# A new order of works and more idle matmuls at the start of a fused linear-attention and softplus MLP kernel

## The chip, the cores and the metric

The kernel runs on one core of a Trainium2 chip. A core has TensorE (PE in the profile), VectorE (DVE), ScalarE (ACT), GpSimd (POOL) and SyncE (SP), which here issues nearly all DMAs. The metric is the device time of one execution in microseconds, the median of several runs.

## The reference

```python
def _attn_ref(q, k, v, omega):          # (8, 8, 576, 64), omega (128, 64)
    scale = 1.0 / np.sqrt(np.sqrt(D))
    q_s, k_s = (q * scale, k * scale)
    def phi(x):
        h = np.einsum('bhsd,md->bhsm', x, omega) - np.sum(x * x, -1, keepdims=True) / 2.0
        return np.exp(h - np.max(h, axis=-1, keepdims=True)) / np.sqrt(m)
    q_p, k_p = (phi(q_s), phi(k_s))
    kv = np.einsum('bhsm,bhsd->bhmd', k_p, v)
    z = np.sum(k_p, axis=2)
    num = np.einsum('bhsm,bhmd->bhsd', q_p, kv)
    den = np.einsum('bhsm,bhm->bhs', q_p, z)[..., None] + 1e-06
    return num / den
def _moe_ref(x, w_in, w_out):           # x (4608, 512), w_in (512, 2048)
    h = x @ w_in
    g = np.maximum(h, 0.0) + np.log1p(np.exp(-np.abs(h)))
    return g @ w_out
```

The output of the attention, with heads side by side, is the x of the MLP.

## The kernel before, in words

The attention is done in 16 quads (8 batches, two halves of the heads each). A quad's keys and queries come in five units of 128 tokens (the last is a tail of 64). For the two quads of batch 0, whose names carry `_0_` and `_1_` in the rows of the order, a key unit is loaded (`xk`), squared on ACT or POOL, projected on PE (`ppk`, L659, in row mode: two 64-row matmuls run side by side), reduced and biased on DVE (`smk`, L649 to L721), exponentiated on ACT (L729) and summed into `kt` on PE (L869). Query units (`xq`, `ppq`) follow in the same way, then transposes (`tpq`), the numerator (`nuq`, L985), the division and the transpose back (`xfq`), which gives the MLP input as a high and a low float32r part (`xh`, `xl`).

The MLP goes in blocks of 512 tokens (the first two of 256). One layer step is twelve matmuls of layer 1 (high by high, high by low, low by high, L1217 to L1219), a softplus on ACT and DVE (`u`, `gh`, `gl`), and three matmuls of layer 2 for each 128 tokens (L1277 to L1279). The weights come raw (`rawi`, `rawo`) and are split into the two parts by ACT, DVE and POOL during the first 100 us.

All of this is cut into some 4,900 works. A work is a piece of program for one engine, with a planned cost. Works are issued in the order of the table `ORDER`: an entry is twice the number of a work, plus one where its second engine is to be taken. A planner (`in_order`, then `timed`) goes through the table with planned costs, among them `START` (when an engine begins), `SLOW` (before this time PE works cost double), `change` (the price of a mode change of PE: plain, row mode "r", column mode "c") and `LULL`/`LULLED` (a pause of SP). It gives out buffers and PSUM banks in that order, so the table sets both who comes first on each engine and which buffer a work waits for. `with_fill` looks at the planned times: where PE is planned to pause it puts in idle matmuls (`fill`, L1733) on a free bank; each is a plain float32 matmul of the identity, which the trace shows as two instructions. Five more stand before the first work, on a zeroed tile `idle`. The planned costs don't run on the chip; only the order, the buffers and the idle matmuls do.

Of the kernel before, what the change touches and what calls it, by code (L numbers as in the profile page):

```python
# [19 lines left out]
P = 128  # L20
S = 576
D = 64
M = 128
NU = 5
DM = 512
# [9 lines left out]
START = {"SP": 0.65, "ACT": 2.1, "PE": 3.4}  # L35
SLOW = 7.9
LULL, LULLED = 20.7, 0.9
# [298 lines left out]
def change(old, new):  # L336

    if old == new:
        return 0.0
    return {("r", None): 0.08, ("c", None): 0, (None, "r"): 0.4, (None, "c"): 0.29}.get((old, new), 0.185)  # L340
# [85 lines left out]
def with_fill(out, held, banks, until, emit):  # L426

    last, all_ = None, []
    for i, w in enumerate(out):
        if w.engine == "PE":  # L430
# [6 lines left out]
            if names and n > 0:  # L437
                all_.append((emit, names[0], n))
# [1404 lines left out]
```

## Time and profile before

| | us |
|---|---|
| median of 3 runs | 993.84 |
| lowest and highest | 993.62 and 993.91 |
| the profiled execution | 996.06 |
| its span, from the first to the last instruction | 994.2 |
| PE busy | 982.4 |
| DVE busy | 799.1 |
| ACT busy | 703.8 |

The span lies 1.9 us below the profiled execution's own time, which lies 2.2 us above the median. Busy times count an engine's instructions as the profile models them; a PE that is busy is not yet one that does useful work, because idle matmuls count too.

### The profile page before, as it was taken

To read this page: it belongs to the slowest core of one execution; us is meant where nothing else is said; L and a number is where in the kernel's file an instruction comes from. 1 tells how busy PE (TensorE), PEld (TensorE's weight loads), DVE (VectorE), ACT (ScalarE), POOL (GpSimd) and SP (SyncE) were. 2 spreads that over 40 slices of the span, in tenths; PEclk is the share of its full clock that TensorE was granted. 3 is DMA by queue.
4 is the path that set the end of the run, shared out by engine and by line. 5 is a ranking of instruction groups with operands and counts; after the bars stand their busy time and mean duration, and the time that the engine had idled before them with its cause. 6 is when DMAs were issued, how large, how long until landed. Compare 5 with 4: busy or idle time off the path is not lost.

```text
span 994.2 us, 17161 instructions
## 1 busy us (share of the span) xinstructions
PE 982.4 (99%) x5553; PEld 808.9 (81%) x5553; DVE 799.1 (80%) x2141; ACT 703.8 (71%) x1708; POOL 314.5 (32%) x284
## 2 busy tenths in 40 slices
PE   9999999999999999999999999999999999999998
PEld 7888888888888788888888888887788778788887
DVE  6999987888888887798889898788877856999620
ACT  5999976768777786877776786877587635775610
POOL 3334333232345333335233431533331212221100
PEclk9999999999999999999999999999999999999999
DMA  9954454334443424342342433343441331000011
GB/s 338 403 188 158 154 152 121 116 110 120 122 130 95 152 77 138 118 139 84 103 150 83 115 117 106 113 134 104 128 133 44 93 109 43 1 1 1 1 32 53
DMA packets 64769, 113.82 MB, mean 114 GB/s; under 512 B 18316, under 2 KB 37672, under 8 KB 64680
## 3 DMA queue, kind: packets, MB, share of 16 engines
q1 hardware_dynamic: 64520, 112.60, 35.8%
q8 instruction: 44, 0.72, 0.3%
q14 instruction: 45, 0.37, 0.1%
q10 hardware_dynamic: 160, 0.13, 0.1%
HBM read 85.68 MB, written 27.03 MB: 113 GB/s over the span
## 4 chain that ended last, share of the span: by engine, by line
PE 83%; DVE 7%; ACT 5%; DMA 3%; issue 1%; SPq 0%; POOL 0%; DVEq 0%; ACTq 0%; POOLq 0%
PE acc L1277 12%; PE acc L1278 12%; PE acc L1279 12%; PE h L1217 10%; PE h L1218 9%; PE h L1219 9%; PE xp L1146 3%; PE kt L824 3%; PE pb L1551 2%; PE ppk L684 2%; PE ppq L684 2%; PE pa L1551 1%; DMA xq<-q 1%; PE pc L1551 1%; PE h L1393 1%
## 5 line engine op out<-in xcount | busy, mean ns | idle before, releaser
L1277 PE MATMUL acc<-wo,gh 128*128 128x512 f32 x512 | 203.6, 398 | 0.1
L1278 PE MATMUL acc<-wo,gh 128*128 128x512 f32 x512 | 200.5, 392 | 0.0
L1279 PE MATMUL acc<-wo,gl 128*128 128x512 f32 x512 | 199.5, 390 | 0.0
L1217 PE MATMUL h<-xh,wi 128*128 128x512 f32 (+1 forms) x512 | 189.2, 369 | 0.5 <-DVE u L1232 0.5
L1218 PE MATMUL h<-xl,wi 128*128 128x512 f32 (+1 forms) x512 | 186.5, 364 | 0.3 <-DVE xl L1018 0.3
L1219 PE MATMUL h<-xh,wi 128*128 128x512 f32 (+1 forms) x512 | 185.7, 363 | 0.0
L1240 POOL TENSOR_TENSOR gl<-u,gh 128x512 fp32r<-128x512 f32 (+1 forms) x74 | 89.0, 1203 | 148.2 <-ACT gh L1236 58.4
L1277 PEld LDWEIGHTS acc<-wo,gh 128*128 128x128 f32 x512 | 96.3, 188 | 22.6 <-issue 4.1
L1217 PEld LDWEIGHTS h<-xh,wi 128*128 128x128 f32 x512 | 96.5, 189 | 20.9 <-issue 3.3
L1279 PEld LDWEIGHTS acc<-wo,gl 128*128 128x128 f32 x512 | 96.1, 188 | 20.8
L1278 PEld LDWEIGHTS acc<-wo,gh 128*128 128x128 f32 x512 | 96.5, 188 | 15.8
L1219 PEld LDWEIGHTS h<-xh,wi 128*128 128x128 f32 x512 | 96.5, 188 | 15.6
L1218 PEld LDWEIGHTS h<-xl,wi 128*128 128x128 f32 x512 | 96.7, 189 | 14.1 <-DVE xl L1018 0.5
L1223 ACT ACTIVATE u<-h 128x512 f32<-128x512 f32 (+1 forms) x128 | 71.3, 558 | 45.8 <-PE h L1219 38.3
L1232 DVE SCALAR_TENSOR_TENSOR u<-h,u 128x512 f32<-128x512 f32 (+1 forms) x128 | 78.0, 616 | 14.9 <-ACT u L1229 13.5
L1065 POOL TENSOR_TENSOR phq<-phq,dnq 128x512 f32<-128x512 f32 x39 | 41.4, 1067 | 135.5 <-DVE dnq L1061 129.6
L1056 DVE CUSTOM_DVE_ANT_0 junk<-phq,zb 128x128 bf16<-128x128 f32 (+1 forms) x228 | 70.6, 310 | 11.2
L1226 ACT ACTIVATE u<-u 128x512 f32<-128x512 f32 (+1 forms) x128 | 75.7, 592 | 2.7
L1229 ACT ACTIVATE u<-u 128x512 f32<-128x512 f32 (+1 forms) x128 | 75.1, 590 | 2.9
L706 ACT ACTIVATE phk<-phk,smk 128x128 f32<-128x128 f32 x208 | 66.7, 391 | 6.7 <-DVE smk L721 6.5
L677 POOL TENSOR_TENSOR spq<-xq,spq 64x512 fp32r<-64x512 f32 (+1 forms) x29 | 37.8, 1304 | 97.7 <-ACT spq L673 78.5
L706 ACT ACTIVATE phq<-phq,smq 128x128 f32<-128x128 f32 x194 | 60.8, 393 | 4.9 <-DVE smq L721 4.8
(221 smaller groups left out, 2021.5 us busy)
## 6 DMA issues: line engine op xcount, KB each, us to landing
xk<-kx SPq DMA_DIRECT2D x28, 512.0 KB, 3.7
xq<-qx SPq DMA_DIRECT2D x28, 512.0 KB, 3.5
fdq<-flq SPq DMA_DIRECT2D x28, 512.0 KB, 2.8
qq<-fdq SPq DMA_DIRECT2D x112, 128.0 KB, 3.0
rawi<-wi SPq DMA_DIRECT2D x16, 512.0 KB, 7.7
rawo<-wo SPq DMA_DIRECT2D x16, 512.0 KB, 5.2
out<-o SPq DMA_DIRECT2D x32, 256.0 KB, 3.2
v<-vv SPq DMA_DIRECT2D x14, 576.0 KB, 4.3
```

The source lines that it names most:

```text
L706: nc.scalar.activation(x, x, AF.Exp, bias=b["sm"][:, 2, c : c + 1])
L1217: nc.tensor.matmul(b["h"], wh, xh[:, cc, t], start=cc == 0, stop=False)
L1218: nc.tensor.matmul(b["h"], wh, xl[:, cc, t], start=False, stop=False)
L1219: nc.tensor.matmul(b["h"], wl, xh[:, cc, t], start=False, stop=cc == NCC - 1)
L1223: nc.scalar.activation(b["u"], b["h"], AF.Abs)
L1226: nc.scalar.activation(b["u"], b["u"], AF.Exp, scale=-1.0)
L1229: nc.scalar.activation(b["u"], b["u"], AF.Ln, bias=1.0)
L1232: nc.vector.scalar_tensor_tensor(b["u"], b["h"], 0.0, b["u"], ALU.max, ALU.add)
L1240: (nc.vector if e == "DVE" else nc.gpsimd).tensor_tensor(b["gl"], b["u"], b["gh"].bitcast(F32), ALU.subtract)
L1277: nc.tensor.matmul(dst, gh, w2[fc][:, 0, c], start=start, stop=False, **kw)
L1278: nc.tensor.matmul(dst, gh, w2[fc][:, 1, c], start=False, stop=False, **kw)
L1279: nc.tensor.matmul(dst, gl, w2[fc][:, 0, c], start=False, stop=stop, **kw)
```

## The change

The change alters four things. The table `ORDER` is replaced as a whole. The planner's prices change: the start of SP, `LULLED`, the mode changes (and these are no longer doubled before `SLOW`), the first big load, and the layer steps, by under 1%. `with_fill` counts idle matmuls otherwise: before `EARLY` one for each 0.2 us of planned pause, without the doubled price; after 16 us the margin is 0.12 us in place of 0.25 us. And an idle matmul that stands between two row-mode works, like the seven (before: five) at the start, takes 64 rows of the identity in place of 128, so that it is of the row mode too.

```diff
-START = {"SP": 0.65, "ACT": 2.1, "PE": 3.4}
+START = {"SP": 0.85, "ACT": 2.1, "PE": 3.4}
 SLOW = 7.9
-LULL, LULLED = 20.7, 0.9
+EARLY = 8.6
+LULL, LULLED = 20.7, 0.5
...
 ORDER = (
-    384, 394, 386, 410, 415, 418, 434, 437, 390, 392, 416, 396, 420, 398, 422, 400, 402, 424, 426, 456, 478, 500, 522,
+    384, 386, 394, 391, 410, 418, 415, 434, 440, 456, 478, 500, 522, 388, 0, 392, 396, 416, 398, 400, 402, 404, 420,
...
-    return {("r", None): 0.08, ("c", None): 0, (None, "r"): 0.4, (None, "c"): 0.29}.get((old, new), 0.185)
+    return {("r", None): 0, ("c", None): 0, (None, "r"): 0.38, (None, "c"): 0.22}.get((old, new), 0.16)
...
-        w.engine, w.cost = e, w.on[e] + (change(mode, w.mode) if e == "PE" else 0)
-        w.cost *= 2 if e == "PE" and t < SLOW else 1
+        w.engine, w.cost = e, w.on[e] * (2 if e == "PE" and t < SLOW else 1)
+        w.cost += change(mode, w.mode) if e == "PE" else 0
...
-    last, all_ = None, []
+    last, mode, all_ = None, None, []
...
-            n = int((t - last - (0.05 if t < 16 else 0.25)) / (0.43 if t < SLOW else 0.224)) if last is not None and t < until else 0
+            n = 0
+            if last is not None and t < until:
+                n = int((t - last) / 0.2) if t < EARLY else int((t - last - (0.05 if t < 16 else 0.12)) / 0.224)
...
-                all_.append((emit, names[0], n))
-            last = w.end
+                all_.append((emit, names[0], n, mode == w.mode == "r"))
+            last, mode = w.end, w.mode
...
-            "SP", dma(P * 4 * cols) + (1.6 if early and kind == "k" and u == 1 and not q.qd else 0), load, behind=prev.get("load"),
+            "SP", dma(P * 4 * cols) + (1.75 if early and kind == "k" and u == 1 and not q.qd else 0), load, behind=prev.get("load"),
...
-                "PE", 0.684, lambda tt=tt: layer2(tt), after=[l, done_w["o", fc]], behind=box.get("l2"),
+                "PE", 0.682, lambda tt=tt: layer2(tt), after=[l, done_w["o", fc]], behind=box.get("l2"),
...
-    def fill(tag, n, idle=ident):
-        t = bank("fill", tag)[:, :P]
+    def fill(tag, n, half, idle=ident):
+        t, x = bank("fill", tag)[:, :P], idle[: D if half else P]
         for _ in range(n):
-            nc.tensor.matmul(t, idle, idle, start=True, stop=True)
+            nc.tensor.matmul(t, x, x, start=True, stop=True)
...
-        fill("at.0", 5, idle)
+        fill("at.0", 7, True, idle)
```

On PE the program begins before as follows. `ppk_a_u` is the projection of key unit u of quad a, four matmuls each, of which two stand here.

```order
L1733 MATMUL fill<-idle 128x128 x5
L659 MATMUL ppk_0_0_0_103<-omf,xk_0_0_101 128x128
...
L659 MATMUL ppk_1_0_0_113<-omf,xk_1_0_110 128x128
...
L1733 MATMUL fill<-ident 128x128 x2
L659 MATMUL ppk_0_1_0_150<-omf,xk_0_1_119 128x128
...
L659 MATMUL ppk_1_1_0_179<-omf,xk_1_1_135 128x128
...
L1733 MATMUL fill<-ident 128x128 x2
L659 MATMUL ppk_0_2_0_188<-omf,xk_0_2_137 128x128
...
L1733 MATMUL fill<-ident 128x128 x4
L659 MATMUL ppk_1_2_0_199<-omf,xk_1_2_139 128x128
```

After the change the same stretch of PE reads:

```order
L1735 MATMUL fill<-idle 128x128 x7
L661 MATMUL ppk_0_0_0_106<-omf,xk_0_0_103 128x128
...
L1735 MATMUL fill<-ident 128x128
L661 MATMUL ppk_1_0_0_117<-omf,xk_1_0_113 128x128
...
L1735 MATMUL fill<-ident 128x128 x9
L661 MATMUL ppk_0_1_0_136<-omf,xk_0_1_124 128x128
...
L661 MATMUL ppk_1_1_0_186<-omf,xk_1_1_142 128x128
...
L1735 MATMUL fill<-ident 128x128 x2
L661 MATMUL ppk_0_2_0_195<-omf,xk_0_2_144 128x128
...
L1735 MATMUL fill<-ident 128x128 x4
L661 MATMUL ppk_1_2_0_214<-omf,xk_1_2_146 128x128
```

The works stand in the same order. There are seven idle matmuls in place of five at the start, one new one between the first two units, and nine in place of two ahead of unit `0_1`; from `1_1` on the idle matmuls are as many as before. Behind these rows both programs have two idle matmuls, `ppk_0_3`, one idle matmul and the first `kt`.

At the first layer step PE has, before, a query projection (`ppq_1_3`) and a transpose ahead of the six matmuls of the first half of layer 1 (`h_0`):

```order
L985 MATMUL nuq_1_0_605<-kvs_1_585,xq_1_0_209 128x65 x4
L985 MATMUL nuq_1_1_612<-kvs_1_585,xq_1_1_273 128x65 x4
L659 MATMUL ppq_1_3_0_620<-omf,xq_1_3_320 128x128
...
L1001 MATMUL xfq_1_0_628<-ident,xq_1_0_209 128x128 x2
L1217 MATMUL h_0_645<-xh,wi_312 128x256
...
L985 MATMUL nuq_0_2_653<-kvs_0_446,xq_0_2_275 128x65 x4
L1001 MATMUL xfq_1_1_661<-ident,xq_1_1_273 128x128 x2
```

After the change the same works stand like this:

```order
L987 MATMUL nuq_1_0_614<-kvs_1_571,xq_1_0_240 128x65 x4
L987 MATMUL nuq_1_1_622<-kvs_1_571,xq_1_1_303 128x65 x4
L987 MATMUL nuq_0_2_627<-kvs_0_460,xq_0_2_305 128x65 x4
L1219 MATMUL h_0_637<-xh,wi_331 128x256
...
L1003 MATMUL xfq_1_0_654<-ident,xq_1_0_240 128x128 x2
L1003 MATMUL xfq_1_1_683<-ident,xq_1_1_303 128x128 x2
L661 MATMUL ppq_1_3_0_687<-omf,xq_1_3_392 128x128
```

Layer 1 begins ahead of the transpose `xfq_1_0` and of `ppq_1_3`, and the numerator of a third query unit has moved up before it.

## Rows read from the trace of the kernel before

**Rows 1.** The page: span; busy time, share and instructions of each engine.

```profile
span 994.2 us, 17161 instructions
...
PE 982.4 (99%) x5553; PEld 808.9 (81%) x5553; DVE 799.1 (80%) x2141; ACT 703.8 (71%) x1708; POOL 314.5 (32%) x284
```

**Rows 2.** Windows; busy us (instructions), then granted clock, DMA share, GB/s.

```profile
8.00:18.00 10.00, 9.83 (x58) 8.24 (x58) 5.33 (x19) 7.33 (x25) 2.89 (x6) 1.00 1.03 401
18.00:27.00 9.00, 8.77 (x77) 7.67 (x76) 8.12 (x29) 6.08 (x19) 3.38 (x5) 1.00 1.04 398
27.00:40.00 13.00, 12.21 (x112) 10.62 (x111) 11.91 (x40) 13.00 (x39) 4.73 (x6) 1.00 1.03 405
40.00:100.00 60.00, 57.51 (x471) 48.95 (x471) 58.01 (x169) 59.58 (x167) 21.94 (x20) 1.00 0.59 210
100.00:500.00 400.00, 399.04 (x2360) 329.67 (x2361) 338.93 (x948) 305.05 (x757) 145.33 (x127) 1.00 0.40 121
500.00:850.00 350.00, 349.21 (x1829) 283.72 (x1828) 286.31 (x764) 241.81 (x572) 111.55 (x95) 1.00 0.34 103
850.00:988.00 138.00, 137.42 (x607) 112.71 (x606) 85.41 (x156) 68.72 (x130) 23.36 (x21) 1.00 0.04 12
```

**Rows 3.** Waits of PE after 100 us: total us, times, longest.

```profile
PE ppk L684 <- DVE spk L677: 0.6, 1, 0.6
PE h L1217 <- DVE u L1232: 0.5, 1, 0.5
PE ppq L684 <- DVE phq L697: 0.4, 2, 0.3
PE ppk L684 <- DVE phk L697: 0.3, 1, 0.3
```

**Rows 4.** Timeline of PE, first 18 us: start, us, instruction, [idle before].

```profile
1.05 2.50 PE L1733 MATMUL fill<-idle 128*128 128x128 f32 x10 [1.05 <-DVE marks L488]
3.94 2.29 PE L659 MATMUL ppk<-omf,xk 64*128 64x128 f32 x16 [0.39 <-DMA xk<-k]
6.16 1.22 PE L1733 MATMUL fill<-ident 128*128 128x128 f32 x4
7.94 2.10 PE L659 MATMUL ppk<-omf,xk 64*128 64x128 f32 x16 [0.56 <-DMA xk<-k]
9.96 1.22 PE L1733 MATMUL fill<-ident 128*128 128x128 f32 x4
11.24 1.29 PE L659 MATMUL ppk<-omf,xk 64*128 64x128 f32 x8
12.46 2.07 PE L1733 MATMUL fill<-ident 128*128 128x128 f32 x8
14.60 1.29 PE L659 MATMUL ppk<-omf,xk 64*128 64x128 f32 x8
15.82 1.13 PE L1733 MATMUL fill<-ident 128*128 128x128 f32 x4
17.01 0.78 PE L659 MATMUL ppk<-omf,xk 64*128 64x128 f32 x8
...
20.20 0.94 PE L659 MATMUL ppk<-omf,xk 64*128 64x128 f32 x12
```

**Rows 5.** Timeline of PE at 59 us: the same idle matmul later.

```profile
59.46 0.83 PE L1733 MATMUL fill<-ident 128*128 128x128 f32 x6
```

**Rows 6.** Timelines of ACT and POOL: squares that start when a load lands.

```profile
7.83 0.42 ACT L642 ACTIVATE xk<-xk 128x256 f32<-128x256 f32 x1 [2.43 <-DMA xk<-k]
...
9.78 0.42 ACT L642 ACTIVATE xk<-xk 128x256 f32<-128x256 f32 x1 [0.51 <-DMA xk<-k]
8.84 0.61 POOL L644 TENSOR_TENSOR xk<-xk 128x256 f32<-128x256 f32 x1 [4.00 <-DMA xk<-k]
10.81 0.61 POOL L644 TENSOR_TENSOR xk<-xk 128x256 f32<-128x256 f32 x1 [1.36 <-DMA xk<-k]
12.10 0.46 ACT L642 ACTIVATE xk<-xk 128x256 f32<-128x256 f32 x1
```

**Rows 7.** Waits of DVE and of ACT between 8 and 27 us.

```profile
DVE smk L709 <- PE ppk L659: 4.9, 5, 1.5
ACT xk L729 <- DVE smk L721: 2.8, 1, 2.8
ACT xk L729 <- PE ppk L659: 1.9, 2, 1.2
```

**Rows 8.** Timeline at the end: the last matmul.

```profile
990.15 0.28 PE L1279 MATMUL right<-wo,g 128*128 128x256 f32 x1
```

More of the change, by code (lines that the diff above doesn't have):

```diff
@@ L346, in in_order @@
     free = {n: (0.0, None) for names in room.values() for n in names}
-    port, mode, lull, out = 0.0, None, LULLED, []
+    port, mode, lull, out = 0.0, "r", LULLED, []
     for k in ORDER:
@@ L386, in timed @@
     clock, head, ready, done = {e: START.get(e, 0.0) for e in queues}, dict.fromkeys(queues, 0), {}, set()
-    ports, mode, lull = {"DVE": -1.0, "POOL": -1.0}, None, LULLED
+    ports, mode, lull = {"DVE": -1.0, "POOL": -1.0}, "r", LULLED
     while len(done) < len(out):
@@ L406, in timed @@
         if e == "PE":
-            w.cost += change(mode, w.mode)
-            w.cost *= 2 if t < SLOW else 1
+            w.cost = w.cost * (2 if t < SLOW else 1) + change(mode, w.mode)
             mode = w.mode
@@ L1250, in plan_step @@
             a = do(
-                "PE", 0.70 if n < TB else 1.36, lambda ccs=ccs: layer1(ccs), after=[x for cc, x in need if cc in ccs] + [done_w["i", fc]], behind=a,
+                "PE", 0.70 if n < TB else 1.37, lambda ccs=ccs: layer1(ccs), after=[x for cc, x in need if cc in ccs] + [done_w["i", fc]], behind=a,
                 take=[] if ccs[0] else [("h", b, "hs")],
@@ L1398, in plan_plain @@
                 a = do(
-                    "PE", 1.36, lambda ccs=ccs: layer1(ccs), after=[x for cc in ccs for x in ready[t][cc]], behind=a,
+                    "PE", 1.37, lambda ccs=ccs: layer1(ccs), after=[x for cc in ccs for x in ready[t][cc]], behind=a,
                     take=[] if ccs[0] else [("h" if t == t7 else "bank", b, "hs")], give=[(w_box["i", fc], "w")] if t == t8 and ccs[0] else [],
@@ L1557, in plan_product @@
                 box["l1"] = do(
-                    "PE", 1.36, lambda: product(k, key, start), after=after, behind=box["l1"],
+                    "PE", 1.37, lambda: product(k, key, start), after=after, behind=box["l1"],
                     take=[("bank", b, ("bank", key))] if start else [], give=give,
@@ L1620, in plan_both @@
                 box["l2"] = do(
-                    "PE", 0.684, lambda tt=tt, fc=fc: layer2(t7, tt, fc), after=[gs[t7, fc][1], done_w["o", fc]],
+                    "PE", 0.682, lambda tt=tt, fc=fc: layer2(t7, tt, fc), after=[gs[t7, fc][1], done_w["o", fc]],
                     behind=box["l2"], take=[] if fc else [("acc", box, ("acc", i, tt))], give=[(gs[t7, fc][0], "gs")] if tt == 3 else [],
@@ L1634, in plan_both @@
             box["l2"] = do(
-                "PE", 0.684 if w == DM else 0.37, lambda tt=tt, fc=fc, c=c: layer2(t8, tt, fc, c),
+                "PE", 0.682 if w == DM else 0.37, lambda tt=tt, fc=fc, c=c: layer2(t8, tt, fc, c),
                 after=[gs[t8, fc][1], done_w["o", fc]], behind=box["l2"],
```

506 rows, old and new, of the table ORDER are left out of this document.

## Prediction

> **What bounds the kernel now.** I read the page first: PE is busy for 982.4 of 994.2 us [rows 1], so the bound is PE, and only time in which PE waits, idles on fill or runs slowly can be won. The windows tell where that is [rows 2]. From 100 to 988 us PE is busy for 399.04 of 400, 349.21 of 350 and 137.42 of 138 us; the four largest waits there come to 1.8 us [rows 3]. The last matmul starts at 990.15 us [rows 8], and the 4 us behind it are the last store, whose instructions the change leaves as they are. So some 2 us lie behind 100 us. From 27 to 100 us ACT is busy for 13.00 of 13 and 59.58 of 60 us, DVE for 11.91 and 58.01, PE for 12.21 and 57.51 [rows 2]: three engines full at once, which a list can rearrange but hardly shorten. What remains is the first 27 us, with ACT busy for 7.33 of 10 and 6.08 of 9 us.
>
> There the timeline of PE shows two things [rows 4]. PE pauses for loads twice, 0.39 us before the first `ppk` and 0.56 us before the unit that starts at 7.94 us. And PE runs slowly for a long time: eight instructions of `ppk` take 1.29 us at 11.24 and at 14.60 us, but 0.78 us at 17.01 us. The idle matmuls say the same, 2.07 us for eight at 12.46 us against 0.83 us for six at 59 us [rows 5]. [...] Ahead of the rise stood the stretch from 7.94 us on, in which the timeline shows no idle time before any group; ahead of that stood the two pauses.
>
> Slow idle matmuls hold PE longer than the loads do. Unit `0_2` lands by 9.78 us and `1_2` by 10.81 us [rows 6], yet their `ppk` start at 11.24 and 14.60 us; `0_3` has landed by 12.10 us and starts at 17.01 us. DVE waits 4.9 us for `ppk` between 8 and 27 us, and ACT waits 2.8 us for the DVE results behind them and 1.9 us for `ppk` itself [rows 7]. So PE's lateness is what holds the head of the program.
>
> **The change part by part.** *The idle matmuls.* The opening in the order: seven in place of five at the start, one more between `ppk_0_0` and `ppk_1_0`, nine in place of two before `ppk_0_1`. At the slow pace one instruction costs (2.50 - 1.22) / 6 = 0.21 us, since ten take 2.50 us and four 1.22 [rows 4]; at the fast pace half of that, 0.11 us, with which the six in 0.83 us agree [rows 5]: five steps are 0.55, and the rest is the length of the last. The trace has no idle matmul on 64 rows; I price it like one on 128, since its columns are as many, and the nearest rows below, the paired `ppk` with 1.29 us for eight and 0.94 us for twelve [rows 4], would make it 0.16 and 0.08 us, but there two share the array, and an idle matmul stands alone.
>
> Step by step: 14 instructions from 1.05 us end at 4.1, so the first `ppk`, which began at 3.94 us, is 0.2 us late. It takes 1.0 us (16 from 7.94 to 9.96 us), the new idle matmul 0.43, `ppk_1_0` 1.0: 6.5 us. The nine are 18 instructions: 1.9 us if the clock has risen, 3.8 us if not, 2.9 us if it rises half way. I take half way, because the two long pauses are gone and PE has by then worked since 1.05 us without one. Then `ppk_0_1` starts at 9.4 us, 1.5 us later than before; this is the price. From there all is at the fast pace: a unit 0.58 us (eight at the 0.94 / 12 of the group at 20.20 us, less the 0.05 by which groups overlap, and no mode change, because the idle matmuls are now of the same mode), an idle matmul 0.21 us. `ppk_0_1` and `ppk_1_1` to 10.6, two idle to 11.0, `ppk_0_2` to 11.6, four idle to 12.4, `ppk_1_2` at 12.4 (before: 14.60), then to 13.0, two idle, `ppk_0_3` at 13.4 us (before: 17.01). Gain at that place: **3.6 us**. With the rise before the nine it is 4.6 us (12.4), with the rise just behind them 2.7 us (14.3).
>
> Can the others follow? DVE's 4.9 us and ACT's 2.8 + 1.9 = 4.7 us of waiting are more than 3.6 [rows 7], and the loads of these units are there [rows 6]. After 27 us all three engines are full [rows 2], so the shift is carried on if the later loads come; the DMA share is 1.03 up to 40 us, but PE takes each unit from `0_2` on 1.5 to 4.9 us after it has landed, so there is room. I carry the whole 3.6 us.
>
> *The new list.* It leaves the order of the first 35 PE rows alone, changes the order at the first layer step, and moves some works between engines, none with a change in PE's work. On PE the work and the number of mode changes stay. What it can win behind 100 us is bounded by the 2 us above; what it can lose has no row, and the nearest are the waits of before, 0.2 to 0.6 us each [rows 3], so I allow 1 us either way and take nothing. The first layer step moves ahead of a transpose and a projection: if its `xh`, `xl` are late, PE waits there as it did for up to 0.6 us elsewhere, inside the same 1 us. *The prices of the planner* do nothing on the chip but through the list and the idle matmuls.
>
> *Sum.* 996.06 - 3.6 = 992.5 us for a profiled execution. The median of before is 2.2 us below its profiled execution. If all of that is a clock that rose earlier in the timed ones, the median has 2.2 of the 3.6 us already and the gain is 1.4; if it is the profiler's, the gain is 3.6. I charge half of it: gain 2.5 us, 993.8 - 2.5 = **991.3 us**.
>
> [...] The moment at which the pace doubles is known here from one execution only. [...]
>
> **The rivals.** *No change:* the timed executions of before have the fast clock early already, or ACT, full from 27 us on, gives the gain back in waits of another kind. For it: the three times lie within 0.29 us, and the profiled one apart from them; and 27 to 100 us leaves PE only 3.3 us of idle time (73 less 12.21 and 57.51). Against: DVE and ACT really wait for PE in the head. Time 992.3 to 994.3, middle 993.3.
>
> *Slower:* the idle matmuls on 64 rows do not bring the clock up. Before, the rise came in a stretch where idle matmuls on 128 rows were issued at 9.96, 12.46 and 15.82 us; after, none stands until the one before `kt`. At the slow pace throughout, `ppk_0_3` starts at 6.5 + 3.8 + 4 x 1.0 + 16 x 0.21 = 17.7 us, 0.7 us later than before, and each microsecond of low clock behind that costs half of one; with 3 to 5 us more it is 2.2 to 3.2 us, 996.0 to 997.0 us. It decides if the rise comes later than about 16.3 us, since the 1.4 us from there, run at the fast pace, make up the 0.7.
>
> *Slower by the list:* the new list has two or three more waits of 0.5 us on PE where PE now has almost none, and the head gains nothing: 994.8 to 995.3 us.
>
> **How the numbers follow.** 0.2% of the time, 2 us, is about what a measurement here can tell from no change. The likeliest case, the gain in the head, has 0.52, with its own range 989.2 to 992.8; seven tenths of it lie below 991.85. No change has 0.33, a fifth of it below 991.85. The slow clock has 0.08 and the list 0.07. Faster: 0.36 + 0.07 = 0.43; slower: 0.08 and a little over half of the list's, 0.12; same: 0.45. The range runs from 989.2 (a gain of 4.6, that of an early rise) to 994.6, which leaves out the slow clock and the worst of the lists.
>
> **What would show it.** Right: after, eight `ppk` instructions take 0.8 us and not 1.29 from `ppk_0_1` or `ppk_1_1` on, `ppk_0_3` starts at 12.4 to 14.3 us, DVE's wait for `ppk` falls from 4.9 us to under 2, ACT is full from about 24 us, and the windows behind 100 us are as full as before. Wrong: the slow pace still at `ppk_0_2`; or the fast pace early, but new waits between 27 and 100 us that eat the 3.6 us; or PE waits behind 100 us of more than 4 us in sum; or a profiled execution 3.6 us shorter beside a median that has not moved, which would say that before's profiled execution was the odd one.

## The result and the profile after

The changed kernel takes 1007.21 us (median of 4, 1005.15 to 1010.58), the kernel before 993.88 us beside it. The ratio is 1.0133, with a 95% interval from 1.0099 to 1.0166: it is 13 us slower. The profiled execution took 1006.0 us. In the experiments below two single executions are far out, 1383 us of the new list alone and 5523 us of the kernel before; no median rests on them. The page of the profiled execution begins, as in [rows 1]:

```profile
span 1004.0 us, 17194 instructions
...
PE 992.2 (99%) x5579; PEld 821.2 (82%) x5579; DVE 799.1 (80%) x2148; ACT 704.7 (70%) x1713; POOL 302.0 (30%) x272
```

The span is 9.8 us longer, and PE is busy for 9.8 us more, with no new work but the idle matmuls. The timeline of PE shows where, read against [rows 4]:

```profile
1.05 3.35 PE L1735 MATMUL fill<-idle 64*128 64x128 f32 x14 [1.05 <-DVE marks L490]
...
7.19 4.05 PE L1735 MATMUL fill<-ident 64*128 64x128 f32 x18
11.29 2.08 PE L661 MATMUL ppk<-omf,xk 64*128 64x128 f32 x16
...
17.26 1.29 PE L661 MATMUL ppk<-omf,xk 64*128 64x128 f32 x8
...
19.40 1.23 PE L661 MATMUL ppk<-omf,xk 64*128 64x128 f32 x8
20.55 0.79 PE L1735 MATMUL fill<-ident 128*128 128x128 f32 x2
21.41 3.68 PE L871 MATMUL kt<-xk 128*128 128x65 f32 x16
...
37.60 2.08 PE L661 MATMUL ppq<-omf,xq 64*128 64x128 f32 x16
...
40.98 1.00 PE L871 MATMUL kt<-xk 128*128 128x65 f32 x8
41.92 0.72 PE L661 MATMUL ppq<-omf,xq 64*128 64x128 f32 x8
42.56 2.00 PE L987 MATMUL nuq<-kvs,xq 128*128 128x65 f32 x16
```

The timeline of before has, behind the rows shown in [rows 4], the first `kt` and the first numerator (`nuq_0_0`):

```profile
18.27 2.00 PE L869 MATMUL kt<-xk 128*128 128x65 f32 x16
...
32.74 1.11 PE L985 MATMUL nuq<-kvs,xq 128*128 128x65 f32 x8
```

Eight instructions of `ppk` still take 1.29 us at 17.26 us and 1.23 us at 19.40 us. The sixteen of the first `kt` take 3.68 us, before 2.00. At 37.60 us sixteen instructions of `ppq` take 2.08 us, as sixteen of `ppk` did at 11.29 us. Only at 40.98 us do eight of `kt` take 1.00 us, half of what sixteen take at the fast pace, and at 41.92 us eight of `ppq` 0.72 us. So PE ran at the slow pace for some 40 us instead of 17, though it hardly paused: the windows, read against [rows 2], have PE full and the other engines waiting.

```profile
18.00:27.00 9.00, 8.88 (x50) 7.73 (x48) 4.75 (x18) 4.22 (x15) 3.01 (x4) 1.00 1.04 401
27.00:40.00 13.00, 13.00 (x74) 11.97 (x74) 7.04 (x28) 7.46 (x22) 1.27 (x1) 1.00 1.03 403
...
100.00:500.00 400.00, 397.75 (x2376) 328.69 (x2373) 339.43 (x962) 304.79 (x765) 146.12 (x127) 1.00 0.40 121
```

From 27 to 40 us PE is busy for all of 13.00 us but gets through 74 instructions, where it got through 112 before. ACT falls from 13.00 us busy to 7.46. The granted clock is printed as 1.00 here too, so only the length of the instructions shows the pace. DVE waits 10.9 us for `ppk` between 8 and 42 us, where the trace of before has 4.9, all of it up to 27 us [rows 7]:

```profile
DVE smk L711 <- PE ppk L661: 10.9, 5, 3.4
```

The first numerator starts at 42.56 us, in the trace of before at 32.74 us: 9.8 us later, as much as the two spans differ. Behind 100 us PE waits a little more than in [rows 3], 3.2 us in three places, where the four largest there had 1.8:

```profile
PE ppq L661 <- DMA xq<-qx: 1.5, 1, 1.5
PE ppk L686 <- DVE phq L699: 1.0, 1, 1.0
PE h L1219 <- DVE u L1234: 0.7, 1, 0.7
```

### The profile page after: what moved, and what is told of

Its sections match the earlier page's. It is cut to its first block, busy times and chain, and to the rows that moved or that the text cites. A ratio compares the mean times of both kernels' runs of the same rounds, so it can differ in the third digit from the quotient of the medians.

```text
span 1004.0 us, 17194 instructions
## 1 busy us (share of the span) xinstructions
PE 992.2 (99%) x5579; PEld 821.2 (82%) x5579; DVE 799.1 (80%) x2148; ACT 704.7 (70%) x1713; POOL 302.0 (30%) x272
## 5 line engine op out<-in xcount | busy, mean ns | idle before, releaser
L1242 POOL TENSOR_TENSOR gl<-u,gh 128x512 fp32r<-128x512 f32 (+1 forms) x78 | 93.9, 1205 | 221.3 <-DVE gh L1238 143.3
L1058 DVE CUSTOM_DVE_ANT_0 junk<-phq,zb 128x128 bf16<-128x128 f32 (+1 forms) x228 | 73.0, 320 | 10.9 <-DVE dnq L1058 0.5
L679 POOL TENSOR_TENSOR spq<-xq,spq 64x512 fp32r<-64x512 f32 (+1 forms) x25 | 32.9, 1315 | 67.8 <-ACT spq L675 49.8
```

The source lines that it names most:

```text
L1058: nc.vector.tensor_tensor_reduce(jk[r, c % jk.shape[1]], ph[r, c], q.zb[r, h], 1.0, 1e-6, ALU.mult, ALU.add, dn[r, 0, c : c + 1])
L1242: (nc.vector if e == "DVE" else nc.gpsimd).tensor_tensor(b["gl"], b["u"], b["gh"].bitcast(F32), ALU.subtract)
```

## The experiments

Theory A was that the idle matmuls on 64 rows leave the pace slow. Theory B was that the list, or the number of idle matmuls, costs the time. Where the expectations speak of the clock, what the traces show is the pace. Times are medians; each ratio is to the kernel before on the same chip, with its 95% interval. Its median was 993.85 to 994.05 us there, most of its executions between 992 and 996 us, so that 0.29 us between three runs had said little.

**All idle matmuls on 128 rows.** Counts and list as in the change.

```diff
-        t, x = bank("fill", tag)[:, :P], idle[: D if half else P]
+        t, x = bank("fill", tag)[:, :P], idle
```

> The changed kernel with every idle matmul on 128 rows; the counts and the list are those of the change. Theory A (idle matmuls on 64 rows leave the clock low): eight ppk instructions take 0.8 us and not 1.29 from 17 us on at the latest, nuq_0_0 starts before 35 us, and the time comes back to 990 to 996 us. Theory B (the 13 us are the new list's, or the number of idle matmuls'): the slow pace may end earlier, but the time stays above 1001 us.

It took 993.3 us, ratio 0.9996 (0.9987 to 1.0006): nearly 14 us less than the change, for the rows alone. The timeline of PE:

```profile
4.34 0.71 PE L661 MATMUL ppk<-omf,xk 64*128 64x128 f32 x8
...
6.18 2.27 PE L1735 MATMUL fill<-ident 128*128 128x128 f32 x18
...
13.78 0.72 PE L661 MATMUL ppk<-omf,xk 64*128 64x128 f32 x8
...
14.97 2.00 PE L871 MATMUL kt<-xk 128*128 128x65 f32 x16
...
28.29 2.00 PE L987 MATMUL nuq<-kvs,xq 128*128 128x65 f32 x16 [0.17 <-ACT xq L979]
```

The fast pace is there at 4.34 us, behind the seven. The first `kt` starts at 14.97 us, 6.4 us earlier than after the change. Theory B falls for the bulk of the loss.

**The kernel before with 64 rows.** Its own list and counts; the size of the identity as in the change.

```diff
-        t = bank("fill", tag)[:, :P]
+        t, x = bank("fill", tag)[:, :P], idle[: D if half else P]
...
-            nc.tensor.matmul(t, idle, idle, start=True, stop=True)
+            nc.tensor.matmul(t, x, x, start=True, stop=True)
...
-        fill("at.0", 5, idle)
+        fill("at.0", 5, True, idle)
```

> The kernel before, its list and its counts, with 64 rows in the five idle matmuls at the start and in those between two row-mode works. Theory A: the slow pace lasts to beyond 30 us and the time is 1002 to 1010 us. Theory B: nothing but saved mode changes, 992 to 995 us.

It took 1000.02 us (998.44 to 1007.27), ratio 1.0080 (1.0045 to 1.0116). The timeline of PE:

```profile
18.43 3.68 PE L869 MATMUL kt<-xk 128*128 128x65 f32 x16
...
28.15 2.08 PE L659 MATMUL ppq<-omf,xq 64*128 64x128 f32 x16
...
33.49 1.16 PE L659 MATMUL ppq<-omf,xq 64*128 64x128 f32 x16
```

`kt` takes 3.68 us, and at 28.15 us sixteen of `ppq` still take 2.08 us; at 33.49 us they take 1.16. So the slow pace lasted beyond 30 us, as theory A had it, and the 64 rows cost 6 us under the old list as well. Fewer of them stand there than in the change, and the cost is smaller; the lower bound of A was 2 us too high.

**The new list alone.** New list and prices, the old rule for the count, 128 rows.

```diff
-            n = 0
-            if last is not None and t < until:
-                n = int((t - last) / 0.2) if t < EARLY else int((t - last - (0.05 if t < 16 else 0.12)) / 0.224)
+            n = int((t - last - (0.05 if t < 16 else 0.25)) / (0.43 if t < SLOW else 0.224)) if last is not None and t < until else 0
...
-        t, x = bank("fill", tag)[:, :P], idle[: D if half else P]
+        t, x = bank("fill", tag)[:, :P], idle
...
-        fill("at.0", 7, True, idle)
+        fill("at.0", 5, True, idle)
```

> The changed list and prices with the old rule for the number of idle matmuls, all on 128 rows (five at the start, four and then two, four, two, one). Theory A: 991 to 995 us, as before, with the fast pace from 12 to 17 us on. Theory B (the list): above 1001 us.

It took 992.46 us, ratio 0.9986 (0.9974 to 0.9999). The list does no harm; by the ratio it is some 1.4 us to the good, with an interval that nearly reaches no change. The timeline of PE:

```profile
6.16 2.07 PE L1733 MATMUL fill<-ident 128*128 128x128 f32 x8
8.29 1.35 PE L659 MATMUL ppk<-omf,xk 64*128 64x128 f32 x16
...
10.35 0.78 PE L659 MATMUL ppk<-omf,xk 64*128 64x128 f32 x8
...
28.07 2.00 PE L985 MATMUL nuq<-kvs,xq 128*128 128x65 f32 x16 [0.18 <-ACT xq L977]
```

Four idle matmuls (eight instructions) at the slow pace, then `ppk` speeds up within the group at 8.29 us: sixteen in 1.35 us, where [rows 4] has 2.10. The first numerator starts 4.7 us earlier than in the trace of before, and the span, 989.7 us, is 4.5 us shorter: here the lead of the head was kept to the end.

**More idle matmuls under the old list.** The new rule for the count, 128 rows, old list.

```diff
+EARLY = 8.6
...
-            n = int((t - last - (0.05 if t < 16 else 0.25)) / (0.43 if t < SLOW else 0.224)) if last is not None and t < until else 0
+            n = 0
+            if last is not None and t < until:
+                n = int((t - last) / 0.2) if t < EARLY else int((t - last - (0.05 if t < 16 else 0.12)) / 0.224)
...
-        fill("at.0", 5, idle)
+        fill("at.0", 7, True, idle)
```

> The old list and prices with the new rule for the number of idle matmuls (seven at the start, five in place of two before ppk_0_1), all on 128 rows. Theory A: the fast pace from 5 to 10 us on and 990 to 993.5 us, since PE is then ahead of where it was by up to 3 us. Rival C (the counts matter, more idle matmuls only delay PE): 994 to 996 us.

It took 995.22 us, ratio 1.0010 (0.9994 to 1.0026): theory A's 990 to 993.5 us missed, rival C fits, though the interval doesn't tell it from no change. In the profiled execution the fast pace did come earlier and the first `kt` started at 16.26 us, 2 us before the 18.27 us of before:

```profile
4.46 2.29 PE L662 MATMUL ppk<-omf,xk 64*128 64x128 f32 x16
...
16.26 2.00 PE L872 MATMUL kt<-xk 128*128 128x65 f32 x16
```

Its span was 993.9 us all the same, where before had 994.2. One wait that the trace of before does not have took most of the 2 us back, at 317 us, for a load of turned queries (PE's waits):

```profile
PE xp L1149 <- DMA qq<-fdq: 1.6, 1, 1.6
```

That is one execution; why the median is no better is open.

**Which of the 64-row matmuls.** First the seven alone on 64 rows, then all but the seven.

```diff
-                all_.append((emit, names[0], n, mode == w.mode == "r"))
+                all_.append((emit, names[0], n, False))
```

> The change with 64 rows in the seven idle matmuls at the start alone; all others on 128 rows. Theory A1 (what matters is what PE runs where the clock could rise, and later idle matmuls on 128 rows raise it): the fast pace begins while the nine run or soon behind them, between 8 and 14 us, and the time is 993 to 996 us. Theory A2 (the first microseconds decide): slow to beyond 17 us, above 998 us.

It took 995.64 us, ratio 1.0015 (0.9999 to 1.0032), as A1 said but at its upper end. The timeline of PE:

```profile
7.62 3.22 PE L1735 MATMUL fill<-ident 128*128 128x128 f32 x18
10.90 1.16 PE L661 MATMUL ppk<-omf,xk 64*128 64x128 f32 x16
```

The eighteen instructions of the nine take 3.22 us, less than the 4.05 at the slow pace, and `ppk` behind them is fast: with later idle matmuls on 128 rows the pace rose, a little late: sixteen in 1.16 us at 10.90 us, where eight had taken 1.22 us at 4.46.

```diff
-        fill("at.0", 7, True, idle)
+        fill("at.0", 7, False, idle)
```

> The change with the seven idle matmuls at the start on 128 rows and those between row-mode works on 64. If once risen the clock stays, it rises at about 4 to 8 us and the time is 990 to 993 us, the best of all since mode changes are saved too. If idle matmuls on 64 rows also let it fall again, or the seven alone are too short to raise it, ppk is slow at 11 to 20 us and the time is 998 to 1008 us.

Both halves of this came true, in different executions. Six of ten took 989.3 to 991.2 us, one 995.5, and three 1002.7 to 1004.7 us; the median, 990.67 us, and the ratio, 0.9997 (0.9958 to 1.0035), mix them. The profiled execution is one of the quick ones:

```profile
4.47 0.72 PE L661 MATMUL ppk<-omf,xk 64*128 64x128 f32 x8
...
6.01 2.17 PE L1735 MATMUL fill<-ident 64*128 64x128 f32 x18
8.24 1.16 PE L661 MATMUL ppk<-omf,xk 64*128 64x128 f32 x16
```

Here the seven brought the fast pace at 4.47 us, and the nine on 64 rows, 2.17 us for 18 instructions, did not end it. The three long ones fit a rise missed there and a slow pace long after: their granted clock is printed as 0.999 to 1.00 (that of the change as 0.998 to 1.00), while the execution with the fall shown in the last section has 0.996; so a fall of that size does not show in them. But no trace shows one of them.

**Both halves of the rows, side by side.** A second idle matmul on rows 64 to 127, into a second bank.

```diff
-                all_.append((emit, names[0], n, mode == w.mode == "r"))
+                all_.append((emit, tuple(names[:2]) if len(names) > 1 else names[0], n, mode == w.mode == "r"))
...
-        t, x = bank("fill", tag)[:, :P], idle[: D if half else P]
-        for _ in range(n):
-            nc.tensor.matmul(t, x, x, start=True, stop=True)
+        pair = isinstance(tag, tuple) and half
+        ts = [bank("fill", x)[:, :P] for x in (tag if pair else [tag[0] if isinstance(tag, tuple) else tag])]
+        for _ in range(n):
+            for j, t in enumerate(ts):
+                x = idle[j * D : (j + 1) * D] if pair else idle
+                nc.tensor.matmul(t, x, x, start=True, stop=True)
...
-        fill("at.0", 7, True, idle)
+        fill(("at.0", "at.1"), 7, True, idle)
```

> The change with a second idle matmul on rows 64 to 127 beside each on rows 0 to 63, into another bank, in the seven at the start and between row-mode works. Theory A3 (what keeps the clock low is the empty half of the array): the pace doubles before 10 us, no mode change is paid, 990.5 to 993 us. Theory A4 (row mode as such does not raise it, side by side or not): slow to beyond 17 us and above 998 us.

It took 990.79 us, ratio 0.9959 (0.9940 to 0.9978), clearly faster than before, and no execution was above 994 us. Theory A4 falls: row mode as such did not keep the pace slow here. The timeline of PE:

```profile
7.17 3.64 PE L1738 MATMUL fill<-ident 64*128 64x128 f32 x36
10.85 1.20 PE L661 MATMUL ppk<-omf,xk 64*128 64x128 f32 x16
```

36 instructions, two at a time (at the fast pace 36 take 2.21 us in the next version with pairs, and 18 single ones 2.27 with all on 128 rows), take 3.64 us, less than the 18 single ones of the change (4.05), since the pace rose while they ran, and the sixteen of `ppk` behind them take 1.20 us. (In this execution the pace rose between 7 and 11 us, not before 10 us for sure.)

**Half of the columns.** The kernel before with 128 rows and 64 columns of weights.

```diff
-        t = bank("fill", tag)[:, :P]
-            nc.tensor.matmul(t, idle, idle, start=True, stop=True)
+        t, x = bank("fill", tag)[: D if half else P, :P], idle[:, : D if half else P]
+            nc.tensor.matmul(t, x, idle, start=True, stop=True)
```

> The kernel before with 128 rows but only 64 columns of weights in the five idle matmuls at the start and in those between row-mode works. Theory A3 (an empty half of the array, whichever): slow to beyond 20 us, 997 to 1008 us, like 64 rows. Theory A5 (only the rows that are fed count): as before, 992 to 996 us.

It took 994.55 us, ratio 1.0001 (0.9988 to 1.0014), as before. Half of the columns stand empty here, where half of the rows did before, yet the pace rose:

```profile
7.70 1.81 PE L659 MATMUL ppk<-omf,xk 64*128 64x128 f32 x16
...
10.15 0.78 PE L659 MATMUL ppk<-omf,xk 64*128 64x128 f32 x8
```

Sixteen of `ppk` at 7.70 us take 1.81 us, eight at 10.15 us 0.78. Theory A3 falls in its wide form: in this kernel empty columns did no harm (ratio 1.0001), empty rows did (1.0080).

**The best of both.** Seven on 128 rows and pairs behind them; then pairs with the old rule for the count and five at the start. The edits are against the version with pairs.

```diff
-        fill(("at.0", "at.1"), 7, True, idle)
+        fill("at.0", 7, False, idle)
```

> The change with the seven idle matmuls at the start on 128 rows, and those between row-mode works in pairs on both halves of the rows. If fed rows are what counts, the clock rises while the seven or the first units run, as with 128 rows everywhere, it can't be missed as with 64 rows later on, and no mode change is paid: 988.5 to 991.5 us with no run above 996. If pairs help only in part, some runs come out above 1000 us.

It took 992.59 us, ratio 0.9985 (0.9970 to 0.9999), with one execution at 997.6: above the 988.5 to 991.5 us that were expected, and not better than pairs throughout.

```diff
-            n = 0
-            if last is not None and t < until:
-                n = int((t - last) / 0.2) if t < EARLY else int((t - last - (0.05 if t < 16 else 0.12)) / 0.224)
+            n = int((t - last - (0.05 if t < 16 else 0.25)) / (0.43 if t < SLOW else 0.224)) if last is not None and t < until else 0
...
-        fill(("at.0", "at.1"), 7, True, idle)
+        fill("at.0", 5, False, idle)
```

> The new list and prices with the old rule for the count (five at the start on 128 rows, then four, two, four, two) and pairs between row-mode works. If the extra idle matmuls only delay the first units, this is 0.5 to 1.5 us better than with seven and nine: 989 to 991.5 us. If they are what raises the clock in time, it is worse, 991.5 to 994 us.

It took 991.92 us, ratio 0.9974 (0.9962 to 0.9987), by 0.4 us in the second of the two ranges. The intervals of the three versions with pairs overlap, so the count is not settled; each is below the kernel before, and some 15 us below the change.

**No idle matmul in the first 30 us.** The kernel before without them.

```diff
+            n = n if t > 30 else 0
             names = names or [box[key] for _, box, key in w.take if box[key] in banks]
...
-        fill("at.0", 5, idle)
```

> The kernel before without any idle matmul in the first 30 us. If idle matmuls on 64 rows are worth nothing for the clock but take time, this is slow to beyond 25 us and 998 to 1006 us, about as with 64 rows in the kernel before (1000.0). If they hold the clock down by themselves, the works alone raise it earlier and this is 994 to 997 us.

It took 996.34 us (991.55 to 999.45), ratio 1.0006 (0.9981 to 1.0030). The median lies in the second branch, but the executions are of two kinds: three took 991.6 to 992.6 us, the profiled one among them, and seven 995.2 to 999.5. In the profiled execution the works alone brought the fast pace with the first `kt`, earlier than with 64-row idle matmuls among them (1000.02 us, slow beyond 30 us); for the longer ones no trace shows it:

```profile
9.05 4.55 PE L660 MATMUL ppk<-omf,xk 64*128 64x128 f32 x32 [0.19 <-DMA xk<-k]
13.54 2.00 PE L870 MATMUL kt<-xk 128*128 128x65 f32 x16
```

32 instructions of `ppk` in a row take 4.55 us, at the slow pace, and `kt` then 2.00 us.

**A burst behind the change.** Sixteen on 128 rows ahead of the first `kt`, all else as in the change.

```diff
+            n = 16 if n > 0 and EARLY < t < 16 and mode == "r" and w.mode != "r" else n
             names = [
```

> The change as it is, but with sixteen idle matmuls on 128 rows in place of one before the first kt. They cost up to 6 us where they stand. If the low clock is the whole loss, the pace doubles while they run, at 22 to 27 us, nuq_0_0 starts at 38 to 41 us and the time is 1001 to 1005 us. If the loss is the list's, the time rises by 3 to 6 us, above 1009 us.

It took 1000.35 us (999.87 to 1000.62), ratio 1.0061 (1.0040 to 1.0082), just below the range for a loss that is all the slow pace's. The timeline of PE:

```profile
20.55 5.55 PE L1736 MATMUL fill<-ident 128*128 128x128 f32 x32
26.16 2.00 PE L872 MATMUL kt<-xk 128*128 128x65 f32 x16
```

The burst holds PE for 5.6 us and `kt` starts 4.8 us later than after the change, but it takes 2.00 us instead of 3.68, and the kernel is 7 us shorter all the same. So the slow pace behind 20 us is the larger part of the loss of 13 us.

## Why the prediction was wrong

*What bounds the kernel* was read rightly: the loss lies in the head, it came from PE's pace, and behind 100 us PE waited under 2 us more than before.

*The step that failed* is the one on the idle matmuls: "I take half way, because the two long pauses are gone and PE has by then worked since 1.05 us without one." The price of one instruction was right, 0.21 us on 64 rows as on 128 (18 in 4.05 us, the last being longer). That a stretch without pauses brings the fast pace was not: with 64 rows PE worked from 1.05 us on with hardly a pause and stayed slow to about 40 us, while 128 rows under the same list and counts had it fast behind the seven (eight of `ppk` in 0.71 us at 4.34 us). I had treated rows as a matter of price alone and put what they do to the pace into a rival with a chance of 0.08. The prediction reckons with a clock that rises or stays low; no run shows such a clock: between 8 and 40 us the windows before and after the change print 1.00 at both paces. What the runs showed in its place is the pace: sixteen of `kt` in 3.68 us or in 2.00.

*The slower rival* was the right mechanism with a term too small. It had `ppk_0_3` at 17.7 us; it started at 19.40 us, since each group of idle matmuls cost about 0.27 us more than its instructions (the four instructions from 18.28 to 19.40 us took 1.12 us, not 0.85), which I had not counted. The first step shows it: by the rows named there, ten in 2.50 us and 0.21 for each of four more, the seven end at 4.40 us and not at 4.1, and so they did. And it had "3 to 5 us more" at the slow pace behind that, for which no row was given; it was 20 us, to between 39.7 and 41.0 us, with a loss of 9.8 us in the profiled execution. The works behind the idle matmuls (`kt`, `ppk`, `ppq`) left the pace slow for all that time, although without any idle matmul ahead of them works alone had brought it up by 13.54 us; why is open. The break-even point of 16.3 us sorts the versions only roughly: those whose profiled execution was fast by then have medians from 3.2 us below the kernel before to 2.3 us above it, and the three others (the change, 64 rows under the old list, the burst) 6 to 13 us above it.

*The gain of 3.6 us in the head* came about in traces with 128 rows, but not in the medians. Under the list and counts of the change `ppk_0_3` started at 13.78 us, where the prediction has 13.4 and before 17.01; the head was 4.5 us ahead at `nuq_0_0` (28.29 against 32.74 us) and the span 2.8 us shorter. A later fall of the granted clock, to 0.57 between 48 and 56 us, took 2.5 us there, as the last section shows; with the new list alone 4.5 of 4.7 us were kept. More idle matmuls under the old list lost their 2 us to a late load. The medians of the three are 0.7 and 1.6 us below the kernel before and 1.2 us above it, so "I carry the whole 3.6 us" is borne out by one trace and by no median. The moment of the rise differed from trace to trace: behind the same seven idle matmuls on 128 rows the first eight of `ppk` took 0.71 and 0.72 us in two of them and 1.02 us in a third, while in a fourth sixteen took 2.29 us. The profiled execution of before fits a late one, and then half of the 2.2 us was too little to charge; no trace of a timed execution shows it.

*The new list* was taken at nothing with 1 us either way; alone it measured -1.4 us by its ratio (0.9974 to 0.9999).

## What to carry to other kernels

In this kernel the sixteen of the first `kt` took 2.00 us behind idle matmuls that fed all 128 rows, either one on all of them or two side by side on the halves, and 3.68 us where all but the last fed 64 alone (the change, and 64 rows under the old list). Elsewhere try the full rows first, and the pair between row-mode works: two idle matmuls and the eight of `ppk` behind them took 1.48 us on 128 rows (9.60 to 11.08 us, list and counts of the change) and 1.21 us in pairs (11.85 to 13.06 us). Before trusting a filler, read the pace of the same work behind it in a trace; a PE that is full and a granted clock printed as 1.00 don't show it: after the change both stood there from 27 to 40 us, with 74 instructions in place of 112. Where the start decides, take ten executions: three that agree say little.

## What the runs showed of the hardware

In the kernel before with half of the columns empty in the idle matmuls the pace was fast at 10.15 us (eight of `ppk` in 0.78 us); with half of the rows empty, in the same places and with the same number of instructions, it was still slow at 28.15 us (sixteen of `ppq` in 2.08 us). After the change PE was busy at the slow pace with real works (`kt`, `ppk`, `ppq`) from 21.41 us on and stayed slow for almost 20 us. Without any idle matmul the works brought the fast pace by 13.54 us, so this is not so of the works as such.

The fast pace was also lost again, in the profiled execution with all idle matmuls on 128 rows. Its windows print a granted clock (third figure from the end) of 1.00 and then of 0.57,

```profile
40.00:48.00 8.00, 7.06 (x55) 5.87 (x53) 7.86 (x29) 8.00 (x24) 4.63 (x4) 1.00 1.03 408
48.00:56.00 8.00, 8.00 (x52) 7.21 (x52) 5.83 (x17) 5.00 (x12) 1.27 (x1) 0.57 0.70 260
```

and at 53.43 us a matmul of layer 1 lasts 0.41 us instead of 0.28:

```profile
42.12 0.28 PE L1219 MATMUL h<-xh,wi 128*128 128x256 f32 x1
...
46.90 0.71 PE L1735 MATMUL fill<-ident 128*128 128x128 f32 x4 [0.78 <-ACT xq L979]
...
53.43 0.41 PE L1219 MATMUL h<-xh,wi 128*128 128x256 f32 x1
...
57.35 0.83 PE L1735 MATMUL fill<-ident 128*128 128x128 f32 x6
```

The new list alone, with the same works in the same order, has at the same two idle matmuls:

```profile
46.98 0.71 PE L1733 MATMUL fill<-ident 128*128 128x128 f32 x4 [0.77 <-ACT xq L977]
...
54.94 0.83 PE L1733 MATMUL fill<-ident 128*128 128x128 f32 x6
```

So the fall cost 2.5 us in this execution: 0.1 us ahead in front of it, 2.4 us behind after it.

Ahead of the fall stood a stretch of small transposes and numerators with a wait of 0.78 us, with PE busy for 7.06 of 8 us. The new list alone had the same stretch with PE busy for 7.09 us, a wait of 0.77 us and no fall (granted clock 1.00 from 40 to 48 and from 48 to 56 us), so what tips it is open.
